# Attention of the first 512 tokens in chunks of 64 tokens, with its state kept on TensorE

## The chip, the cores and the metric

The kernel runs on one core of one Trainium2 chip. The metric is the device time of one execution in microseconds, taken as the median of several runs. The kernel before takes 574.92 us (three runs, 574.86 to 575.62).

## The reference

A linear attention with a decay per head (2 batch entries, 8 heads, 768 tokens, head size 64) gives 1536 rows of 512 features. Two wide layers follow (512 to 2048 to 512), the first with an ELU, the second with a rational function of the hidden value.

```python
for b in range(nb):                      # blocks of 64 tokens
    intra = einsum('bhic,bhjc->bhij', qb, kb) * Dmask      # lam**(i-j) for i >= j, else 0
    intra = einsum('bhij,bhjd->bhid', intra, vb)
    inter = einsum('bhid,bhde->bhie', qb * lam_pow, kv_state)
    out[:, :, sl] = intra + inter
    kv_state = lam_block * kv_state + einsum('bhsd,bhse->bhde', kb * rev_pow, vb)
x = out.transpose(0, 2, 1, 3).reshape(B * S, H * D)
x = elu(x @ w_in) @ w_out
h = x @ w2_in;  P = a0 + a1 h + a2 h^2 + a3 h^3;  Q = 1 + |b0||h| + |b1| h^2
y = (P / (Q + 1e-6)) @ w2_out
```

## The kernel before

The 1536 tokens are three tiles of T = 512. For each layer and tile, 16 slices f of 128 hidden features are computed: `mlp_h` (line 441) makes the hidden slice `h` with 12 products of 512 columns, `mlp_y` (line 523) adds it to the four output sums `y` with 12 more. Each operand is split into a high and a low part, and the three products high·high, high·low and low·high are summed, so `x` exists as `xhi` and `xlo`, and a weight as `w[:, 0]` and `w[:, 1]`. The split is a copy on ScalarE (line 57) and a subtraction on VectorE (line 58).

Attention is done twice over. For tiles 1 and 2 it runs inside the first layer: at chosen slices f (`visits`) `sm_products` does one chunk of 64 tokens between two groups of MLP products, with 64x64 operands in the tile names `aa`. For tile 0 it runs ahead of everything, in eight groups (c, g): c is one of four chunks of 128 tokens, g one of two groups of four heads. Per group TensorE makes the scores (`att_s`, line 209), and in `att_av` the products with the values (line 241), with the state (line 247) and the new state (line 254). GpSimd scales keys and queries (`att_kq`, lines 214 and 220), VectorE multiplies the scores by the decay mask (line 226), adds to the state (line 284) and makes `xlo` (line 277); ScalarE writes `xhi` (lines 263 and 269) and fades the state (line 266). `att_hand` (line 293) moves the state to the other half of the partitions for the later chunks.

Everything up to the third tile is written inside `manual_schedule`, so each engine runs its instructions in the order of the code. Loads are issued on SyncE (SP) in code order: the 16 pieces of queries, keys and values (line 192, 256 KB each) with the raw weight halves (line 114) between them. The raw weights are 64-bit floats, which VectorE narrows in three steps (lines 78, 81, 84); then they are split (lines 127 and 128). `idle` issues products of zeros on TensorE.

At the turn from tile 0 to tile 1, ScalarE stands in this order: the last chunk's output (line 390), the fade of the next chunk's keys (line 371, in `sm_decay_k`), a weight split (line 127), and the four splits of the new `x` (line 57), which the first `mlp_h` of tile 1 needs.

Of the kernel before, what the change touches and what calls it, by code (L numbers as in the profile page):

```python
# [29 lines left out]
def fused_kernel(ctx, tc, lam, qkv, w1, w2, ab, out):  # L30
# [132 lines left out]
    def make_w2(f, i):  # L163
# [5 lines left out]
        else:  # L169
# [5 lines left out]
    group = {}  # L175

    VIEWS = ("p (a x i) -> p a x i", "p (a x e) -> p a x e",
             "p (h a i) -> p h a i", "p (x a i) -> p x a i")

    def att_tile(c, g, j):  # L180

        b = group.setdefault((c, g), {})
        if j not in b:
            if j == 0:
                b["all"] = slot(2 + len(group) - 1, [P, 4, DM], F32, f"att{c}_{g}")
            b[j] = b["all"][:, j].rearrange(
                VIEWS[j], **({"h": 2, "a": 2} if j == 2 else {"a": 2, "x": 2}))
        return b[j]

    def att_load(c, g, parts=(0, 1)):  # L190
        for j in parts:
            nc.sync.dma_start(out=att_tile(c, g, j).rearrange("p a x i -> p (a x i)"),  # L192
                              in_=qkv[c, g, j])

    def psum_tiles(psum, name):
        return [pool.tile([P, T], F32, tag=tag, name=f"pa{h2}_{name}")
                .rearrange("p (a i) -> p a i", a=4) for h2, (pool, tag) in enumerate(psum)]

    def att_psum(c, g, psum):
        group[c, g]["ps"] = psum_tiles(psum, f"{c}_{g}")  # L200

    def att_s(c, g, psum):
        if "ps" not in group[c, g]:
            att_psum(c, g, psum)
        qk, ps = group[c, g][0], group[c, g]["ps"]
        for a in range(2):
            for h2 in range(2):
                r = slice(h2 * D, (h2 + 1) * D)
                nc.tensor.matmul(ps[h2][:, a], lhsT=qk[r, a, 1], rhs=qk[r, a, 0],  # L209
                                 start=True, stop=True)  # L210

    def att_kq(c, g):
        qk, kv, kq = group[c, g][0], att_tile(c, g, 1), att_tile(c, g, 3)
        nc.gpsimd.tensor_tensor(
            out=kq[:, 0].rearrange("p a (h d) -> p a h d", h=2),
            in0=kv[:, :, 0].rearrange("p a (h d) -> p a h d", h=2),
            in1=dmask[:, 4 * g:4 * g + 4, C - 1:C].rearrange("p (a h) i -> p a h i", h=2)
            .to_broadcast([P, 2, 2, D]), op=ALU.mult)
        if c:
            nc.gpsimd.tensor_tensor(out=kq[:, 1], in0=qk[:, :, 0], in1=qpow[:, 2 * g:2 * g + 2],  # L220
                                    op=ALU.mult)

    def att_mask(c, g):
        s, ps = att_tile(c, g, 2), group[c, g]["ps"]
        for h2 in range(2):
            nc.vector.tensor_tensor(
                out=s[:, h2], in0=ps[h2][:, 0:2],
                in1=dmask[:, 4 * g:4 * g + 4, 0:C].rearrange("p (a h) i -> p h a i", h=2)[:, h2],
                op=ALU.mult)

    def att_av(c, g):
        b = group[c, g]
        kv, s, kq, ps = b[1], b[2], b[3], b["ps"]
        first, last = c == 0, c == NC - 1
        pu = ps[1][:, 2].rearrange("p (a e) -> p a e", a=2)


        for a in range(2):
            for h2 in range(2):
                r = slice(h2 * D, (h2 + 1) * D)  # L240
                nc.tensor.matmul(ps[0][r, 2 + a], lhsT=kv[:, a, 1, r], rhs=s[:, h2, a],  # L241
                                 start=a == 0, stop=first, skip_group_check=True)
        if not first:
            for a in range(2):
                for h2 in range(2):
                    r = slice(h2 * D, (h2 + 1) * D)
                    nc.tensor.matmul(ps[0][r, 2 + a], lhsT=state[:, 2 * g + a, h2],  # L247
                                     rhs=kq[:, 1, a], start=False, stop=True,
                                     skip_group_check=True)
        for a in range(2):  # L250
            for h2 in range(2):
                r = slice(h2 * D, (h2 + 1) * D)
                ro = slice((1 - h2) * D, (2 - h2) * D) if last else r
                nc.tensor.matmul(pu[ro, a], lhsT=kq[:, 0, a, r], rhs=kv[:, a, 1, r],  # L254
                                 start=a == 0 or not last, stop=not last, skip_group_check=True)
        js = slice(c * C, (c + 1) * C)

        if c == 0:
            x_tiles(0, 0, g)
        hi, lo = xg[0, 0, g]  # L260
        gs_ = slice(2 * g, 2 * g + 2)
        if last:
            nc.scalar.activation(out=hi[:, :, js], in_=ps[0][:, 2:4], func=AF.Copy)
        if not first:
            for a in range(2):
                nc.scalar.activation(out=state[:, 2 * g + a], in_=state[:, 2 * g + a],
                                     func=AF.Copy, scale=qpow[:, 2 * g + a, C - 1:C])
        if not last:
            nc.scalar.activation(out=hi[:, :, js], in_=ps[0][:, 2:4], func=AF.Copy)
        if first:  # L270
            for h2 in range(2):
                r = slice(h2 * D, (h2 + 1) * D)
                nc.scalar.activation(out=state[r, gs_, h2, :], in_=pu[r], func=AF.Copy)

    def att_low(c, g):
        js, ps, (hi, lo) = slice(c * C, (c + 1) * C), group[c, g]["ps"], xg[0, 0, g]
        nc.vector.tensor_tensor(out=lo[:, :, js], in0=ps[0][:, 2:4],
                                in1=hi[:, :, js].bitcast(F32), op=ALU.subtract)

    def att_add(c, g):  # L280
        pu = group[c, g]["ps"][1][:, 2].rearrange("p (a e) -> p a e", a=2)
        for h2 in range(2):
            r = slice(h2 * D, (h2 + 1) * D)
            nc.vector.tensor_tensor(out=state[r, 2 * g:2 * g + 2, h2, :], in0=pu[r],
                                    in1=state[r, 2 * g:2 * g + 2, h2, :], op=ALU.add)

    def att_hand(c, g):

        pu = group[c, g]["ps"][1][:, 2].rearrange("p (a e) -> p a e", a=2)
        for a in range(2):  # L290
            for h2 in range(2):
                ro = slice((1 - h2) * D, (2 - h2) * D)
                nc.tensor.matmul(pu[ro, a], lhsT=ident, rhs=state[:, 2 * g + a, h2],  # L293
                                 start=False, stop=True, skip_group_check=True)
        nc.scalar.activation(out=state[:, 2 * g:2 * g + 2, 0], in_=pu, func=AF.Copy)

# [5 lines left out]

    def sm_load_qk(k):

        c, row = k // 2, 4 * P  # L310
        qk = qq.tile([P, NP, 2, C], F32, tag="qk", name=f"qk{c}")
        src = qkv[c, 0, 0]
        for rho, r in enumerate(ROWS):
            nc.sync.dma_start(
                out=qk[r].rearrange("p (g a) x i -> p g (a x i)", a=2),
                in_=bass.AP(src.tensor, src.offset + (1 - rho) * D * row,
                            [[row, D], [2 * P * row, NP // 2], [1, row]]))
# [14 lines left out]

    def sm_products(n, d):
# [40 lines left out]
    def sm_decay_q(n):  # L374
        q = chunk[n]["q"]
        if n % KB:
            nc.gpsimd.tensor_tensor(out=q, in0=q, in1=qpow[:, :, 0:CS], op=ALU.mult)

    def sm_mask(n):
        b = chunk[n]  # L380
        b["s"] = s = ap_.tile([P, NP, CS], F32, tag="s", name=f"s{n}")
        nc.vector.tensor_tensor(out=s, in0=aa_tiles[0][:, 0], in1=mask64[:, :, 0:CS], op=ALU.mult)
# [29 lines left out]
    def x_tiles(layer, t, g):  # L412
        key = f"{layer}_{t}_{g}"
        pool = xp if layer == 0 or t % 2 else xq
        xg[layer, t, g] = [pool.tile([P, 2, T], F32R, tag=f"x{w}{g}", name=f"x{w}{key}")
# [4 lines left out]
    def x_split(layer, t, m):  # L420
        with tc.high_priority(HP):
            if m % 2 == 0:
                x_tiles(layer, t, m // 2)
# [467 lines left out]
```

## Time and profile before

| | us |
|---|---|
| median of three runs | 574.92 |
| the profiled execution, its own time | 575.37 |
| its span, first to last instruction | 573.6 |
| start of the first MLP product (line 441) | 23.21 |
| TensorE busy in the span | 566.7 |

The span is read in two parts. Up to 23.21 us the core works on the attention of tile 0; behind that TensorE runs MLP products without a gap worth naming until near the end. The granted TensorE clock reads 1.00 over the whole span. A time on the page is of one instruction's whole length, and products overlap, so the distance from one start to the next tells the rate and not the length. A product in full fp32 is two instructions on TensorE in the trace, so 16 steps are 8 products of the code.

### The profile page before, as it was taken

The numbers are of one execution on the slowest core, as the hardware profiler recorded it, in microseconds if no ns is written. First come the engines' busy times: TensorE is split into PE (matmuls) and PEld (weight loads), VectorE is DVE, ScalarE is ACT, GpSimd is POOL, SyncE is SP. The second block draws the span as 40 slices with busy tenths as digits, with TensorE's granted clock in tenths as the row PEclk, the third lists the DMA queues.
The fourth block names the chain that finished last, engine by engine and source line by source line (L and its number), as shares of the span: only waits on it lengthen the run. The fifth ranks groups of instructions, "written<-read, shape, count | busy, mean of one in ns | idle before, by whom it ended". The sixth has DMA issues, their size and how long they took to land.

```text
span 573.6 us, 9267 instructions
## 1 busy us (share of the span) xinstructions
PE 566.7 (99%) x3554; PEld 465.8 (81%) x3554; DVE 467.6 (82%) x730; ACT 356.7 (62%) x682; POOL 27.5 (5%) x51
## 2 busy tenths in 40 slices
PE   7999999999999999999999999999999999999997
PEld 6878888878888888888888888888888888888885
DVE  6999999965586626877979999888898888898882
ACT  2565645865454445556568977667886676776672
POOL 6300000100010000000000000000000000000000
PEclk9999999999999999999999999999999999999999
DMA  8877687365778603544533400000300000200001
GB/s 296 274 237 260 209 251 221 83 164 161 221 216 244 185 11 125 183 142 156 175 99 103 162 22 2 0 1 1 129 18 2 0 1 0 75 0 2 0 1 74
DMA packets 41215, 64.58 MB, mean 113 GB/s; under 512 B 20178, under 2 KB 20178, under 8 KB 41170
## 3 DMA queue, kind: packets, MB, share of 16 engines
q1 hardware_dynamic: 41170, 63.98, 35.5%
q8 instruction: 28, 0.46, 0.3%
q14 instruction: 17, 0.14, 0.1%
HBM read 53.48 MB, written 10.49 MB: 112 GB/s over the span
## 4 chain that ended last, share of the span: by engine, by line
PE 97%; DMA 1%; SPq 1%; issue 0%; ACT 0%
PE h L441 46%; PE y L523 43%; PE y L432 3%; PE aa L346 1%; DMA att<-qkv_in 1%; PE aa L357 1%; SPq L192 1%; PE pa L241 1%; PE pa L247 1%; PE pa L209 0%; PE aa L362 0%; PE aa L351 0%; PE pa L254 0%; PE pa L293 0%; ACT o L493 0%
## 5 line engine op out<-in xcount | busy, mean ns | idle before, releaser
L441 PE MATMUL h<-xhi,w 128*128 128x512 f32 x768 | 205.7, 390 | 0.1
L523 PE MATMUL y<-ghi,w 128*128 128x512 f32 x712 | 191.8, 392 | 0.0
L441 PEld LDWEIGHTS h<-xhi,w 128*128 128x128 f32 x768 | 143.9, 188 | 31.2 <-ACT xhi L57 1.3
L523 PEld LDWEIGHTS y<-ghi,w 128*128 128x128 f32 x712 | 132.3, 188 | 27.8
L441 PE MATMUL h<-xlo,w 128*128 128x512 f32 x384 | 102.7, 389 | 0.0
L523 PE MATMUL y<-glo,w 128*128 128x512 f32 x356 | 95.3, 389 | 0.0
L441 PEld LDWEIGHTS h<-xlo,w 128*128 128x128 f32 x384 | 72.1, 188 | 15.2 <-DVE xlo L58 0.2
L523 PEld LDWEIGHTS y<-glo,w 128*128 128x128 f32 x356 | 66.8, 188 | 14.2
L467 ACT ACTIVATE a<-h,babs 128x512 f32<-128x512 f32 x48 | 33.0, 688 | 63.9 <-PE h L441 63.7
L454 ACT ACTIVATE a<-h 128x512 f32<-128x512 f32 x48 | 28.2, 589 | 48.3 <-PE h L441 48.2
L471 DVE SCALAR_TENSOR_TENSOR b<-b,babs,a 128x512 f32<-128x512 f32 x48 | 36.0, 750 | 21.2 <-ACT b L468 21.1
L456 DVE SCALAR_TENSOR_TENSOR b<-a,h 128x512 f32<-128x512 f32 x48 | 32.7, 681 | 17.1 <-ACT a L455 14.1
L458 ACT ACTIVATE ghi<-b 128x512 fp32r<-128x512 f32 x48 | 30.0, 626 | 19.0 <-DVE b L456 19.0
L459 DVE TENSOR_TENSOR glo<-b,ghi 128x512 fp32r<-128x512 f32 x48 | 33.9, 708 | 7.0 <-ACT ghi L458 5.5
L469 ACT ACTIVATE p<-h,cab 128x512 f32<-128x512 f32 x48 | 37.6, 784 | 0.0
L473 ACT ACTIVATE a<-b,one 128x512 f32<-128x512 f32 x48 | 34.9, 728 | 3.2 <-DVE b L471 2.7
L475 DVE SCALAR_TENSOR_TENSOR p<-p,cab,h 128x512 f32<-128x512 f32 x48 | 35.8, 746 | 1.2
L479 DVE SCALAR_TENSOR_TENSOR b<-b,one,a 128x512 f32<-128x512 f32 x48 | 35.8, 746 | 0.1
L481 DVE SCALAR_TENSOR_TENSOR p<-p,cab,a 128x512 f32<-128x512 f32 x48 | 35.8, 746 | 0.0
L58 DVE TENSOR_TENSOR glo<-p,ghi 128x512 fp32r<-128x512 f32 x48 | 33.0, 687 | 3.1 <-PE y L432 1.5
L474 DVE TENSOR_TENSOR p<-p,h 128x512 f32<-128x512 f32 x48 | 32.7, 681 | 2.9 <-ACT p L469 2.9
L483 DVE SCALAR_TENSOR_TENSOR p<-b,p 128x512 f32<-128x512 f32 x48 | 33.1, 690 | 1.2
(87 smaller groups left out, 612.4 us busy)
## 6 DMA issues: line engine op xcount, KB each, us to landing
raw<-w_in SPq DMA_DIRECT2D x64, 512.0 KB, 4.3
att<-qkv_in SPq DMA_DIRECT2D x16, 256.0 KB, 5.8
qk<-qkv_in SPq DMA_DIRECT2D x16, 256.0 KB, 4.1
kv<-qkv_in SPq DMA_DIRECT2D x64, 64.0 KB, 3.9
w2d<-wbuf SPq DMA_DIRECT2D x16, 256.0 KB, 4.4
wbuf<-w2d SPq DMA_DIRECT2D x16, 256.0 KB, 2.7
x2d<-o SPq DMA_DIRECT2D x12, 256.0 KB, 2.2
x2r<-x2d SPq DMA_DIRECT2D x12, 256.0 KB, 3.1
```

The source lines that it names most:

```text
L58: lo_eng.tensor_tensor(out=lo, in0=src, in1=hi.bitcast(F32), op=ALU.subtract)
L441: nc.tensor.matmul(h, lhsT=w[:, a, 0, k * P:(k + 1) * P], rhs=xs[layer, t, k][b], start=i == k == 0, stop=i == 2 and k == NP - 1)
L459: lambda: nc.vector.tensor_tensor(out=glo, in0=b, in1=ghi.bitcast(F32), op=ALU.subtract)]
L467: nc.scalar.activation(out=a, in_=h, func=AF.Abs, scale=babs[:, 0:1])
L469: nc.scalar.activation(out=p, in_=h, func=AF.Identity, scale=cab[:, 3:4], bias=cab[:, 2:3])
L471: nc.vector.scalar_tensor_tensor(out=b, in0=b, scalar=babs[:, 1:2], in1=a, op0=ALU.mult, op1=ALU.add)
L473: nc.scalar.activation(out=a, in_=b, func=AF.Ln, bias=one[:, 0:1])
L475: nc.vector.scalar_tensor_tensor(out=p, in0=p, scalar=cab[:, 1:2], in1=h, op0=ALU.add, op1=ALU.mult)
L479: nc.vector.scalar_tensor_tensor(out=b, in0=b, scalar=one[:, 0:1], in1=a, op0=ALU.add, op1=ALU.mult)
L481: nc.vector.scalar_tensor_tensor(out=p, in0=p, scalar=cab[:, 0:1], in1=a, op0=ALU.add, op1=ALU.mult)
L483: nc.vector.scalar_tensor_tensor(out=p, in0=b, scalar=2.0, in1=p, op0=ALU.subtract, op1=ALU.mult, reverse0=True)
L523: nc.tensor.matmul(ys[layer, t][m], lhsT=w[:, a, 1, m * P:(m + 1) * P], rhs=g[b], start=f == i == 0, stop=False)
```

## The change

The attention of tile 0 works in chunks of 64 tokens. One piece holds two chunks b = 0, 1 of all eight heads; its keys and values stand in opposite halves of the partitions. All products have 64x64 operands. The state is carried in PSUM: `att_kv` makes the new part, `att_fade` adds the old state times a diagonal `fade`, and ScalarE copies the sum out (`att_state`) for the next chunk. `att_inter` multiplies the state by the faded queries. Where products of different row halves write into one bank, `fence` makes the next product wait for a tiny ScalarE instruction (`mark`), which waits for the last product.

The loads come as eight pieces of 512 KB: queries and keys of c = 0, a raw weight half, the values of c = 0 and 1, and so on; the queries of c = 2 and 3 are last. The `x` tiles become one tile for all four feature groups. For the very first hidden slice the order of the parts is high·high, low·high, high·low. The tables of powers are made on GpSimd (`make_qpow` twice), so the two products of line 339 and `pick` go. `att_hand` goes: the last `att_fade` does its work. At the turn to tile 1 the fade of the keys is issued behind the splits of `x`.

```diff
-            for r in ROWS:
-                nc.tensor.matmul(aa_tiles[1][r, 1], lhsT=pick[r], rhs=mask64[r, :, 1:CS + 1],
-                                 start=True, stop=True, skip_group_check=True)
-            nc.scalar.activation(out=qpow[:, :, 0:CS], in_=aa_tiles[1][:, 1], func=AF.Copy)
...
+    def mark():
+        i = nc.scalar.activation(out=marks[0:1, 0:1], in_=one[0:1], func=AF.Copy)
+        order(i, pe["last"])
+        return i
+    def fence(i):
+        pe["after"] = i
...
+    def att_kd(c):
+        t = att[c]
+        for g in range(2):
+            gm = slice(2 * g, 2 * g + 2)
+            nc.gpsimd.tensor_tensor(
+                out=t["kd"][:, gm].rearrange("p m (h d) -> p m h d", h=2),
+                in0=t["kv"][:, gm, 0].rearrange("p m (h d) -> p m h d", h=2),
+                in1=dmask[:, 4 * g:4 * g + 4, CS - 1:CS].rearrange("p (m h) i -> p m h i", h=2)
+                .to_broadcast([P, 2, 2, D]), op=ALU.mult)
+    def att_qd(c, b, eng):
+        t, j = att[c], slice(b * CS, (b + 1) * CS)
+        eng.tensor_tensor(out=t["qd"][:, :, j], in0=t["qk"][:, :, 0, j], in1=qnat, op=ALU.mult)
+    def att_av(c, bs=(0, 1)):
+        t = att[c]
+        for m in range(NP):
+            for h2, e in enumerate(ROWS):
+                for b in bs:
+                    att_mm(t["px"][b][e, m], lhsT=t["kv"][ROWS[1 - b], m, 1, e],
+                           rhs=t["s"][ROWS[1 - b], h2, m], start=False, stop=c > 0 or b == 0)
+    def att_kv(c):
+        t = att[c]
+        for m in range(NP):
+            for h2, e in enumerate(ROWS):
+                for b in (1, 0):
+                    o = ROWS[1 - h2] if (c, b) == (NC - 1, 1) else e
+                    att_mm(t["pu"][b][o, m], lhsT=t["kd"][ROWS[1 - b], m, e],
+                           rhs=t["kv"][ROWS[1 - b], m, 1, e], start=m == 0, stop=c == b == 0)
+    def att_inter(c, b):
+        t, p = att[c], plane(2 * c + b)
+        for m in range(NP):
+            for r in ROWS:
+                att_mm(t["px"][b][r, m], lhsT=p[r, m], rhs=t["qd"][r, m, b * CS:(b + 1) * CS],
+                       start=False, stop=not c)
+    def att_fade(c, b):
+        t, p = att[c], plane(2 * c + b)
+        for m in range(NP):
+            for i, r in enumerate(ROWS):
+                att_mm(t["pu"][b][ROWS[1 - i] if (c, b) == (NC - 1, 1) else r, m],
+                       lhsT=fade[r, m], rhs=p[r, m], start=False, stop=True)
+    def att_state(c, b):
+        return nc.scalar.activation(out=plane(2 * c + b + 1), in_=att[c]["pu"][b], func=AF.Copy)
...
+            att_kd(0); att_qd(0, 1, G); att_av(0); att_hi(0, 0); att_low(0, 0)
+            idle(2); att_kv(0); idle(1); att_state(0, 0)
...
+            att_inter(0, 1); att_fade(0, 1); att_state(0, 1); att_hi(0, 1)
...
+            att_s(1, ms); att_mask(1, 0); att_mask(1, 1); att_low(0, 1)
+            att_qd(1, 0, G); att_qd(1, 1, V); att_kv(1)
+            fence(mark())
+            att_fade(1, 0); att_inter(1, 0); att_state(1, 0); att_kd(2)
+            att_fade(1, 1); att_inter(1, 1); f = att_state(1, 1)
+            att_av(1, (0,)); fence(f); att_av(1, (1,)); att_hi(1, 0); att_hi(1, 1)
...
+            att_kv(2); fence(mark()); att_fade(2, 0); att_state(2, 0)
+            att_kv(3); att_fade(2, 1); att_state(2, 1)
+            att_qd(2, 0, G); att_qd(2, 1, V); att_s(2, ms[:2])
+            att_inter(2, 0); att_inter(2, 1); att_s(2, ms[2:])
+            att_mask(2, 0); att_mask(2, 1); att_fade(3, 0); att_state(3, 0)
...
+            att_s(3, ms); att_mask(3, 0); att_mask(3, 1); att_av(2); att_hi(2, 0); att_hi(2, 1)
...
+            att_inter(3, 0); att_inter(3, 1); fence(mark())
+            att_av(3); att_hi(3, 0); att_hi(3, 1); att_low(3, 0); att_low(3, 1)
...
                     for m in range(NP):
                         x_split(0, t, m)
+                    for n in due:
+                        sm_decay_k(n)
...
                     for n in due:
-                        sm_decay_k(n)
+                        if f < NF - 1:
+                            sm_decay_k(n)
```

(Several calls stand on one line here.) The next two excerpts are of TensorE, in the middle of the attention of tile 0; names that begin with `pa` or `ps` are sums in PSUM, `att` are tiles in SBUF. First before, from the products of the group (2, 0) on:

```order
L241 MATMUL pa_2_0_305<-att_0_178 64x128 x4
L247 MATMUL pa_2_0_305<-att_0_178,state 64x128 x4
L254 MATMUL pa_2_0_306<-att_0_178 64x64 x4
L209 MATMUL pa_3_1_392<-att_1_188 128x128
L209 MATMUL pa_3_1_393<-att_1_188 128x128
L209 MATMUL pa_3_1_392<-att_1_188 128x128
L209 MATMUL pa_3_1_393<-att_1_188 128x128
L241 MATMUL pa_2_1_333<-att_1_180 64x128 x4
```

Now the change, behind `att_kv(1)`: fade and inter of chunk (1, 0), the same of (1, 1), and the two halves of `att_av(1)`.

```order
L213 MATMUL ps_2_323<-att_0_138,att_2_142 64x64 x8
L213 MATMUL ps_2_323<-att_1_140,att_0_138 64x64 x8
L213 MATMUL ps_3_324<-att_1_140,att_2_142 64x64 x8
L213 MATMUL ps_3_324<-att_1_140 64x64 x8
L213 MATMUL ps_2_323<-att_1_140,att_1_139 64x64 x8
L213 MATMUL ps_3_324<-att_1_140,att_1_139 64x64 x8
```

Groups of four products with 128 columns, whose state is added elsewhere, become groups of eight products with 64 columns; the second row's sum stands in the bank of the first, and the third row reads the state that comes out of it.

ScalarE at the turn from tile 0 to tile 1, before:

```order
L390 ACTIVATE xr_764<-aa_614 128x4x64
L371 ACTIVATE kv_1445<-kv_1445,dmask 128x64 x4
L127 ACTIVATE w_15_235<-wbuf 128x512
L57 ACTIVATE xhi_1_0_1568<-xr_764 128x512 x2
L57 ACTIVATE xhi_1_1_1574<-xr_764 128x512 x2
L458 ACTIVATE ghi_0_15_1475<-b_0_15_1478 128x512
```

And now (`xr` is the attention's output, `kv` the loaded keys and values):

```order
L400 ACTIVATE xr_920<-aa_773 128x4x64
L127 ACTIVATE w_15_229<-wbuf 128x512
L57 ACTIVATE xhi_1_1720<-xr_920 128x512 x4
L381 ACTIVATE kv_1601<-kv_1601,mask_164 128x64 x4
L467 ACTIVATE ghi_0_15_1631<-b_0_15_1634 128x512
```

The four fades of the keys, which wait for a load, have moved from ahead of the splits to behind them.

## Rows read from the trace of the kernel before

**Rows 1.** The page: busy time by engine, and the chain by line.

```profile
PE 566.7 (99%) x3554; PEld 465.8 (81%) x3554; DVE 467.6 (82%) x730; ACT 356.7 (62%) x682; POOL 27.5 (5%) x51
PE h L441 46%; PE y L523 43%; PE y L432 3%; PE aa L346 1%; DMA att<-qkv_in 1%; PE aa L357 1%; SPq L192 1%; PE pa L241 1%; PE pa L247 1%; PE pa L209 0%; PE aa L362 0%; PE aa L351 0%; PE pa L254 0%; PE pa L293 0%; ACT o L493 0%
```

**Rows 2.** The chain in order of time (start, length, what) to 39 us.

```profile
28.95 0.38 PE pa L293 x8
...
32.27 2.72 PE y L523 x12
34.99 2.89 PE h L441 x12
...
38.47 0.46 PE aa L346 x16
```

**Rows 3.** Timeline of TensorE (start, length, operation, shapes, count, idle before).

```profile
4.76 2.08 PE L209 MATMUL pa<-att 64*128 64x128 f32 x16
...
8.18 0.72 PE L209 MATMUL pa<-att 64*128 64x128 f32 x8
...
22.54 0.27 PE L247 MATMUL pa<-att,state 128*64 128x128 f32 x1
...
23.21 1.20 PE L441 MATMUL h<-xhi,w 128*128 128x512 f32 x4
```

**Rows 4.** Timeline of GpSimd, the scaled keys and queries.

```profile
7.61 0.62 POOL L214 TENSOR_TENSOR att<-att,dmask 128x256 f32<-128x256 f32 x1 [0.19 <-DMA att<-qkv_in]
9.56 0.62 POOL L214 TENSOR_TENSOR att<-att,dmask 128x256 f32<-128x256 f32 x1 [1.33 <-DMA att<-qkv_in]
...
15.00 0.61 POOL L214 TENSOR_TENSOR att<-att,dmask 128x256 f32<-128x256 f32 x1
15.58 0.72 POOL L220 TENSOR_TENSOR att<-att,qpow 128x256 f32<-128x256 f32 x1
```

**Rows 5.** Timeline of ScalarE at the end of the attention of tile 0.

```profile
21.55 0.38 ACT L263 ACTIVATE xhi<-pa 128x256 fp32r<-128x256 f32 x1 [0.72 <-PE pa L247]
21.83 0.69 ACT L266 ACTIVATE state<-state,qpow 128x128 f32<-128x128 f32 x2
22.85 0.39 ACT L263 ACTIVATE xhi<-pa 128x256 fp32r<-128x256 f32 x1 [0.34 <-PE pa L247]
...
25.15 0.19 ACT L693 ACTIVATE babs<-cab 128x2 f32<-128x2 f32 x1
```

**Rows 6.** Timeline of TensorE around the visits at 38 and 114 us.

```profile
37.82 0.65 PE L339 MATMUL aa<-dmask,tabs 64*64 64x256 f32 x4
38.30 0.63 PE L346 MATMUL aa<-qk 64*64 64x64 f32 x16
...
113.59 0.27 PE L346 MATMUL aa<-qk 64*64 64x64 f32 x2
...
114.53 0.23 PE L362 MATMUL aa<-qk,state 64*64 64x64 f32 x2
```

**Rows 7.** The chain in order of time at the turn to tile 1.

```profile
120.42 0.34 PE h L441
...
121.83 4.20 PE h L441 x17
```

**Rows 8.** Timelines of ScalarE and, last row, VectorE at the turn to tile 1.

```profile
115.78 0.37 ACT L390 ACTIVATE xr<-aa 128x256 f32<-128x256 f32 x1
118.11 1.07 ACT L371 ACTIVATE kv<-kv,dmask 128x64 f32<-128x64 f32 x4 [1.96 <-DMA kv<-qkv_in]
...
119.60 2.18 ACT L57 ACTIVATE xhi<-xr 128x512 fp32r<-128x512 f32 x4
...
120.25 2.50 DVE L58 TENSOR_TENSOR xlo<-xr,xhi 128x512 fp32r<-128x512 f32 x4 [3.38 <-ACT xhi L57]
```

**Rows 9.** Windows: busy by engine (TensorE, loads, VectorE, ScalarE, GpSimd), granted clock, DMA.

```profile
4.00:8.00 4.00, 4.00 (x36) 3.41 (x35) 3.74 (x11) 0.12 (x1) 3.28 (x9) 1.00 0.93 286
8.00:12.00 4.00, 2.25 (x34) 1.80 (x32) 2.88 (x7) 1.51 (x6) 2.67 (x5) 1.00 1.04 401
```

More of the change, by code (lines that the diff above doesn't have):

```diff
@@ L190, in att_load @@
[L190 to L295, printed above, removed]
     CS = D
@@ L331, in sm_load_kv, with att_mm, order @@
                     [[row, CS], [P, 4], [1, D]]))
+    att = []
+    pe = {"last": None, "after": None}
+    def att_mm(out, **kw):
+        i = nc.tensor.matmul(out, skip_group_check=True, **kw)
+        if pe["after"] is not None:
+            order(i, pe["after"])
+        pe.update(last=i, after=None)
+    def order(i, j):
+        tc.add_manual_dep(i.ins, j.ins.name,
+                          mybir.DependencyInfo(mybir.DependencyClass.Sync, mybir.DependencyReason.DATA),
+                          reason="row tiles of one bank")
@@ new lines, in att_psum, with att_s @@
+    def att_psum(c):
+        pools = (((ph, "h"), (ph, "h"), (pa, "pa0"), (pa, "pa1")), ((py, "y"),) * 4)[c % 2]
+        ps = [pool.tile([P, T], F32, tag=tag, name=f"ps{c}_{i}")
+              .rearrange("p (x m i) -> p x m i", x=2, m=NP) for i, (pool, tag) in enumerate(pools)]
+        x = 2 if c else 0
+        att[c].update(ps=[ps[i][:, 0] for i in range(2)], pu=[ps[2 + i][:, 0] for i in range(2)],
+                      px=[ps[i + x][:, 1] for i in range(2)])
+    def att_s(c, ms):
+        t = att[c]
+        for m in ms:
+            for b in range(2):
+                for h2, r in enumerate(ROWS):
+                    att_mm(t["ps"][h2][ROWS[1 - b], m], lhsT=t["qk"][r, m, 1, (1 - b) * CS:(2 - b) * CS],
+                           rhs=t["qk"][r, m, 0, b * CS:(b + 1) * CS], start=True, stop=True)
@@ L555, in fused_kernel @@
+        dmask = att[3]["spare"].rearrange("p (h i) -> p h i", h=H)
+        fade = att[2]["spare"].rearrange("p (x m i) -> p x m i", x=2, m=NP)[:, 0]
+        qnat = att[2]["spare"].rearrange("p (x m i) -> p x m i", x=2, m=NP)[:, 1]
+        ident = ap_.tile([P, NP, CS], F32, tag="s", name="ident")[:, 0]
         for last in (D - 1, P - 1):
-            nc.gpsimd.affine_select(out=pick, in_=pick, pattern=[[0, D]], base=-last,
+            nc.gpsimd.affine_select(out=diag, in_=diag, pattern=[[1, CS]], base=-last,
@@ L625, in run, with idle @@
                         ops.pop(0)()
-            att_psum(*atts[0], pp[0])
-            idle(3, group[atts[0]]["ps"])
-            pl = group[atts[0]]["ps"][0][:, 3, 0:H]
-            nc.tensor.matmul(pl, lhsT=zero[0:1, P:2 * P], rhs=lam1, start=True, stop=True)
+            x_tiles(0, 0)
+            att_psum(0)
+            spare = py.tile([P, T], F32, tag="y", name="spare")
+            def idle(n, out=spare):
+                for _ in range(n):
+                    nc.tensor.matmul(out[:, 0:P], lhsT=zero[:, 0:P], rhs=zero[:, 0:P],
+                                     start=True, stop=True, skip_group_check=True)
@@ L631, in fused_kernel @@
+            idle(3)
+            pl = spare[:, P:P + H]
+            nc.tensor.matmul(pl, lhsT=zero[0:1, P:2 * P], rhs=lam1, start=True, stop=True,
+                             skip_group_check=True)
             nc.vector.tensor_copy(out=lamb, in_=pl)
[L632 removed]
+            idle(3)
             for h in range(H):
                 make_decay(h)
[L635 to L640 removed]
@@ L675, in fused_kernel @@
-            s_part(7)
-            masks(7)
-            av(5)
-            add(5)
-            low(5)
-            av(6)
-            low(6)
-            run(c1, 1)
-            av(7)
-            low(7)
-            run(c1, 2)
-            att_hand(*atts[6])
+            V, G, ms = nc.vector, nc.gpsimd, range(NP)
+            att_s(0, ms)
+            att_mask(0, 0)
+            att_mask(0, 1)
+            idle(5)
+            run(c0, 3)
+            att_kd(0)
+            att_qd(0, 1, G)
+            att_av(0)
@@ new lines, in fused_kernel @@
+            att_hi(0, 0)
+            att_low(0, 0)
+            idle(2)
+            att_kv(0)
+            idle(1)
+            att_state(0, 0)
+            run(c0, 1)
+            att_kd(1)
+            att_inter(0, 1)
+            att_fade(0, 1)
+            att_state(0, 1)
+            att_hi(0, 1)
+            run(c0, 1)
+            att_psum(1)
+            att_s(1, ms)
+            att_mask(1, 0)
+            att_mask(1, 1)
+            att_low(0, 1)
+            att_qd(1, 0, G)
+            att_qd(1, 1, V)
@@ new lines, in fused_kernel @@
+            att_kv(1)
+            fence(mark())
+            att_fade(1, 0)
+            att_inter(1, 0)
+            att_state(1, 0)
+            att_kd(2)
+            att_fade(1, 1)
+            att_inter(1, 1)
+            f = att_state(1, 1)
+            att_av(1, (0,))
+            fence(f)
+            att_av(1, (1,))
+            att_hi(1, 0)
+            att_hi(1, 1)
+            run(c1, 3)
+            att_low(1, 0)
+            att_low(1, 1)
+            att_kd(3)
+            att_psum(2)
@@ new lines, in fused_kernel @@
+            att_kv(2)
+            fence(mark())
+            att_fade(2, 0)
+            att_state(2, 0)
+            att_psum(3)
+            att_kv(3)
+            att_fade(2, 1)
+            att_state(2, 1)
+            att_qd(2, 0, G)
+            att_qd(2, 1, V)
+            att_s(2, ms[:2])
+            att_inter(2, 0)
+            att_inter(2, 1)
+            att_s(2, ms[2:])
+            att_mask(2, 0)
+            att_mask(2, 1)
+            att_fade(3, 0)
+            att_state(3, 0)
@@ new lines, in fused_kernel @@
+            run(c1, 1)
+            att_qd(3, 0, G)
+            att_qd(3, 1, V)
+            att_s(3, ms)
+            att_mask(3, 0)
+            att_mask(3, 1)
+            att_av(2)
+            att_hi(2, 0)
+            att_hi(2, 1)
+            run(c1, 1)
+            att_low(2, 0)
+            att_low(2, 1)
+            att_inter(3, 0)
+            att_inter(3, 1)
+            fence(mark())
+            att_av(3)
+            att_hi(3, 0)
+            att_hi(3, 1)
+            att_low(3, 0)
```

198 lines of the change are left out of this document (92 added, 106 removed).

## The prediction

> **What bounds the kernel now.** I read the page first: TensorE is busy for 566.7 of 573.6 us, and the chain that ended last is nearly all MLP products [rows 1]. So only two things can move the end: when the first MLP product starts, and holes in the row of products behind it. Next I read the chain in order of time. The first MLP product starts at 23.21 [rows 3], and behind it the chain is products on TensorE alone, the hand's and the visits' among them [rows 2]. Then the timelines of that first stage engine by engine: TensorE [rows 3], GpSimd [rows 4] and ScalarE [rows 5]. The reader is to see that GpSimd waits there for pieces of the load, and that TensorE, at the stage's end, waits on turns through ScalarE. Then the visits [rows 6] and the turn to tile 1 [rows 7, 8]. There ScalarE stands 1.96 us before the faded keys, waiting for their load, while the splits of `x` stand behind them. Last the granted clock by window [rows 9].
>
> **The scale.** The profiled execution took 575.37, 1.77 over its span and 0.45 over the median of 574.92. I sum on 575.37 and take 0.45 off. This kernel's measurement can't tell a difference below 0.2% (1.15 us) from none.
>
> **Part 1: the attention of tile 0.** It is now one long queue on TensorE, and I work out its end S, which is the start of the first MLP product, against 23.21.
>
> *When it can start.* Scores of c = 0 need only the first load. The first link that holds up the queue is `att_kv(0)`, which needs the faded keys. Before, GpSimd waits for the fourth 256 KB piece of the load until 7.61 and for the seventh until 9.56 [rows 4]: 0.65 us a piece. Now the values of c = 0 come behind the queries (two pieces' bytes) and a raw half (two more), so they are complete with the sixth piece's bytes: 9.56 - 0.65 = 8.9. A raw half has longer lines, and if lines and not bytes set the pace, it counts as one piece: 8.3. The keys' fade is two GpSimd instructions of 128x256: 0.58 from one start to the next and 0.62 for the last [rows 4], with 0.05 to hand it on: 1.25. The queue starts at 10.15 by bytes and at 9.55 by lines.
>
> *The products.* A visit's 16 steps of 64x64, eight products in fp32 on two quarters of the array, take 0.46 [rows 2]. A visit of 64 steps, which uses all four quarters, starts its first two at 113.59 and its last two at 114.53 [rows 6]: 0.94 for 62, so 0.48 for 32 steps, 16 products. A group thus costs 0.47, whether it is eight products on two quarters or 16 on four. Behind the start I count 24 such groups ahead of the first MLP product: one `att_kv` for c = 0 to 3 (4), `att_inter` of seven chunks (7), `att_fade` of six (6), `att_s` of c = 1 to 3 (3), `att_av` of c = 1 in two halves and of c = 2 and 3 (4). 24 x 0.47 = 11.3.
>
> *The turns.* Where TensorE needs what ScalarE makes of the last product, it stands. From the start of a last product to ScalarE is 22.54 to 22.85 [rows 3, 5]: 0.27 length and 0.04 hand-over; I take 0.16 for the shorter 64-column product. A copy of 128x256 from PSUM takes 0.38, with 0.28 to the next start [rows 5]; 0.05 back to TensorE. A state turn is then 0.16 + 0.04 + 0.38 + 0.05 = 0.63. A mark is a tiny instruction, as the 0.19 of 128x2 [rows 5]: 0.16 + 0.04 + 0.19 + 0.05 = 0.44. By the order of the code these lie on the path: the states of (0, 0) and (1, 0), bare, 1.26; the first and the last mark 0.88; the middle mark with the copies of `xhi` that stand ahead of it on ScalarE 0.55; the fence on the state of (1, 1), half covered by a half `att_av`, 0.25; the state of (2, 0) behind `att_kv(3)` and the masks of c = 3 behind VectorE's other work, 0.1 each; and the last pair of `xhi` copies, which the first MLP product waits for, 0.16 + 0.04 + 0.28 + 0.38 + 0.05 = 0.91. Sum 4.05. The other turns lie under products of another chunk. If all but the last pair and two state turns were hidden, it would be 2.2.
>
> S = 10.15 + 11.3 + 4.05 = 25.5 by bytes, 24.9 by lines; I take the middle, 25.2. The bounds: 9.55 + 11.3 + 2.2 = 23.1 (by lines, turns hidden), and 26.4 (by bytes, with GpSimd's fade a quarter slower, +0.3, and as much, +0.6, on the 2.5 of ScalarE's work in the turns, as both go on beside VectorE's narrowing). The queries of c = 2 and 3, though loaded last, come before 19 by the same pace; they are not needed until some 18 to 20. So part 1 costs +2.0, bounds -0.1 and +3.2.
>
> At the marks a rule speaks against the change. Rows 6 show no wait for ScalarE within a visit, so on rows alone a mark could cost nothing where its product has drained. The Trainium skill ("TensorEngine Tiling (Array Packing)", Restrictions and Gotchas) says that row tiles can't use one PSUM bank at the same time and that the program has to keep them apart. By it the three marks are needed and cost up to 3 x 0.44 = 1.3; without it S could be 1.3 lower, which lies inside the bounds above.
>
> **Part 2: what is saved later.** The products of line 339 stand on TensorE's path at 37.82, and the visit starts at 38.30 [rows 6]: -0.48. The tables that replace them are made on GpSimd behind the attention, needed at the first visit some 13 us later; GpSimd is busy 27.5 us of the span [rows 1], which hides them (bare, ten instructions of at most 0.62 [rows 4] would be 6.2). The second slice's third group of products took 2.89 for 2.72 [rows 2], a wait for a weight: with a later start of the products, VectorE's narrowing is ahead of them, -0.17. The hand's eight steps of 0.38 [rows 2] become a fade of 16 steps: +0.09.
>
> At the turn to tile 1 the chain shows 20 products from 120.42 to 126.03 (three alone, then 17) [rows 7]: 5.61, where 20 at 2.72 / 12 take 4.53 [rows 2]: a hole of 1.08. ScalarE's splits there start at 119.60, behind the keys' fade that waited for its load until 118.11 [rows 8]. With the fade behind them they follow the output of 115.78 and one weight split, two microseconds earlier; TensorE needs them at 120.42, so the hole goes: -1.08. Next late is the gelu's copy behind the fade; with four fades of 1.07 in all it is ready within the slice's 5.4 us, so I cost the new place at 0 (if the load came 2 us later still, up to +0.5).
>
> Larger loads move the same bytes and one order of parts in the first slice takes no product away: 0, within -0.2 and +0.3.
>
> **Sum.** +2.0 - 0.48 - 0.17 + 0.09 - 1.08 = +0.36: 575.7 on the profiled scale, 575.3 by the median.
>
> **The rivals.**
>
> *B, the turns hide, faster.* If TensorE finds other products in nearly every turn, S is near its lower bound, say 23.4, and the sum +0.2 - 1.64 = -1.44: 573.5. For it: the 11.3 of products has independent groups, and before, the chain is mostly load and TensorE. Against it: the state goes from chunk to chunk eight times in series, each through ScalarE.
>
> *C, doubled products, slower.* Before, 16 steps of 64x128 at 4.76 take 2.08, and at 8.18 eight take 0.72 [rows 3], 0.21 against 0.11 a pair of starts, although the granted clock of both windows reads 1.00, the level of 2.4 GHz [rows 9]. If the early rate lasts until about 13 because the new first stage waits more than it works, the four groups `att_inter`, `att_fade`, `att_s` and `att_kv` there take 0.94 for 0.47: +1.9, 577.2. It decides if products started after 9 still take the doubled time. Against it: at 8.18 the rate had already changed, in a window in which TensorE was busy for only 2.25 of 4 us [rows 3, 9]. The Trainium skill ("TensorE: Matmul & The Clock Gate", Part 1) says that the clock starts at half and that work releases it, and idling takes it back; the row of the granted clock does not show a half level here, so the rule has only the doubled steps for it.
>
> *D, the move at the turn does nothing*, because the splits now wait for the weight split and VectorE's narrowing ahead of it: the hole stays, +1.08, 576.4. Against it: VectorE sat idle for 3.38 before its part of the splits, waiting for ScalarE [rows 8], so its narrowing was done.
>
> **Chances.** Forecast 0.48. B 0.25, from the lower bound of the turns. C 0.13. D 0.05. The upper end of part 1 (S above 25.9) 0.09, which is slower too. So faster 0.25, same 0.48, slower 0.27. The range runs from 573.4, B's time with a little more, to 577.1, just short of C; the forecast's own is 574.4 to 576.1.
>
> **What would show it.** The first product of an MLP slice at 25.2 (B: 23.4; C: 27). GpSimd's first fade of keys at 8.3 to 8.9. Gaps of TensorE of about 0.4 ahead of the products behind the three marks, and of 0.6 behind the copies of the states of (0, 0) and (1, 0). Groups of 64x64 at 0.47 from 10 us on (C: 0.94 until 13). No product ahead of the first visit's scores. Slice 0 of tile 1 with 12 products in 2.72, and its splits before 119. I am wrong if the first MLP product comes before 24 or after 26.5, or if a new hole opens behind it.

## The result and the profile after

The kernel got slower, clear of noise. The prediction of 575.3 us, with a range from 573.4 to 577.1, missed it.

| | before | after |
|---|---|---|
| median of four runs, us | 575.04 | 583.50 |
| ratio of after to before, 95% interval | | 1.0133 (1.0113 to 1.0153) |
| span of the profiled execution, us | 573.6 | 581.6 |
| start of the first MLP product, us | 23.21 | 32.06 |
| from there to the first product of tile 1, us | 97.06 | 96.70 |
| the 24 products of the first two slices of tile 1, us | 6.51 | 5.99 |
| from there to the end, us | 443.19 | 443.19 |

The last four rows add up to the end of the last product, some 3.6 us ahead of the span's end in both. Behind the first MLP product the change gains 0.36 and 0.52, where 0.56 and 1.08 were forecast. Ahead of it the change loses 8.85, where +2.0 was forecast. So nearly all that went wrong happened in the first 32 us.

The chain in order of time tells where. These are pieces of it in the changed kernel (start, length, what; "issue" is time in which the engine waited for nothing that the profile shows):

```profile
10.59 0.02 issue
...
10.67 0.39 ACT att L331
11.07 0.14 issue
11.20 2.05 PE ps L213 x91
13.25 1.55 issue
14.80 0.23 PE ps L213
15.03 0.02 issue
15.05 0.21 ACT marks L226
15.26 0.04 issue
15.30 1.89 PE ps L213 x32
...
17.71 2.12 PE ps L213 x44
...
21.01 0.08 issue
21.09 0.28 PE ps L213
...
22.93 2.08 PE ps L213 x72
25.02 2.33 issue
27.35 2.58 PE ps L213 x110
...
30.71 0.10 issue
30.81 0.52 PE ps L213 x15
31.33 0.02 issue
31.35 0.67 ACT xhi L339 x2
32.02 0.04 issue
32.06 0.97 PE h L450 x3
```

The reader is to see two long pieces with no releaser, 1.55 and 2.33, and two short ones that end at 21.09 and 30.81, all inside rows of products. The ones that end at 14.80 and 21.09 stand just ahead of the product that a mark waits for, so this view alone does not tell whether they belong to the marks; the run pad below does. The turns are a little longer than forecast: the state turn takes 0.61 from the end of its last product at 10.59 to 11.20, where the forecast 0.63 counts 0.16 of that product too and so leaves 0.47, and the first mark takes 0.50 from 14.80 to 15.30 (0.44 was forecast).

What the four places have in common appears when the span is cut there and TensorE's instructions are counted (windows of the changed kernel: stretch, length, then busy time and instructions of TensorE's products, of its weight loads, of VectorE, ScalarE and GpSimd, granted clock, DMA share, GB/s):

```profile
0.00:14.79 14.79, 11.67 (x221) 10.26 (x222) 8.64 (x25) 3.23 (x6) 10.37 (x27) 1.00 0.84 318
14.79:21.09 6.29, 5.36 (x128) 4.69 (x127) 1.76 (x4) 1.74 (x5) 4.31 (x11) 0.73 1.04 399
21.09:27.34 6.25, 3.50 (x127) 3.08 (x127) 1.19 (x3) 0.97 (x3) 1.34 (x4) 1.00 0.82 155
27.34:30.81 3.47, 3.01 (x127) 2.73 (x128) 2.78 (x7) 1.76 (x5) 0.00 (x0) 1.00 0.02 5
```

Products and loads of the last three stretches are 255, 254 and 255; with the few waits for semaphores that the trace lists among them, each comes to 256, and the first stretch to 449. TensorE stands each time that 256 instructions are through, at the counts 449, 705, 961 and 1217. A product in full fp32 is two weight loads and two products here, four instructions, so the chunks need 1244 products and loads ahead of the first MLP product. Before, it is 524:

```profile
0.00:23.20 23.20, 19.98 (x262) 17.61 (x262) 17.90 (x49) 8.72 (x25) 14.77 (x36) 1.00 0.93 326
```

Instructions are data too, and come by DMA. This is the table of queues of the changed kernel's whole execution (packets, MB, share):

```profile
q1 hardware_dynamic: 41042, 63.98, 34.9%
q8 instruction: 30, 0.49, 0.4%
q14 instruction: 16, 0.13, 0.1%
```

TensorE's 7886 traced instructions over the 30 packets of q8 are 263 a packet, and a packet is 16 KB, so q8 is taken to be TensorE's queue. In the trace such a packet starts at 12.46, 18.53, 24.23 and 28.54, always behind the passing of one of the counts (193 at 9.87, then 14.80, 21.09, 27.34), and TensorE goes on some 1.2 to 1.6 us after the packet's end. So it looks as if a block is asked for when the block two before it is used up; it is there 4.9, 6.3, 6.25 and 3.5 us later. The last of them, without other loads, is the short one. The Trainium skill ("Runtime: NRT & Kernel Launch", Instruction fetch mechanics) states blocks of 256 instructions, fetched over a queue while the one before runs; the counts agree. It gives TensorE room for 2048 instructions and calls the cost of a block's end mostly hidden; here TensorE stood at its instruction 449, and the measurement decides.

The clock is a second effect of the same stalls. The first stage of the changed kernel by windows, same columns:

```profile
12.00:14.00 2.00, 1.25 (x75) 1.15 (x72) 2.00 (x5) 0.66 (x2) 1.93 (x3) 1.00 1.03 377
16.00:18.00 2.00, 1.46 (x29) 1.28 (x28) 0.08 (x1) 0.38 (x1) 1.83 (x3) 0.50 1.05 410
18.00:20.00 2.00, 1.98 (x52) 1.84 (x51) 0.00 (x0) 0.51 (x2) 1.35 (x5) 0.78 1.04 391
```

After the stall of 1.55 the granted clock falls from 1.00 to 0.50, the level of 1.2 GHz. The 32 steps from 15.30 take 1.89; the same 32 take 1.15 in the run hold_pad below, at the full clock. It cost little here, since the next block came only at 21.09. (A window shows the clock only where the trace has a record of it. The records begin at 8.63 here and at 7.29 before; a window without a record reads 1.00.)

### The profile page after: what moved, and what is told of

Read it like the earlier page. It is cut to its first block, busy times and chain, and to the rows that moved or that the text cites. A ratio compares the mean times of both kernels' runs of the same rounds, so it can differ in the third digit from the quotient of the medians.

```text
span 581.6 us, 9939 instructions
## 1 busy us (share of the span) xinstructions
PE 570.0 (98%) x3918; PEld 469.4 (81%) x3918; DVE 463.4 (80%) x717; ACT 354.6 (61%) x674; POOL 31.3 (5%) x56
## 4 chain that ended last, share of the span: by engine, by line
PE 98%; issue 1%; ACT 1%; DVE 0%; ACTq 0%
PE h L450 45%; PE y L532 42%; PE y L441 3%; PE ps L213 3%; PE aa L356 1%; PE spare L626 1%; PE aa L367 1%; PE aa L372 0%; PE aa L361 0%; ACT att L331 0%; ACT xhi L339 0%; ACT marks L226 0%; ACT o L502 0%; PE spare L631 0%; DVE lamb L633 0%
```

## Experiments

The ratios are to the runs of before on the same chip, with their 95% interval; pad, hold and hold_pad have two runs each.

| run | time, us | ratio to before | first MLP product, us |
|---|---|---|---|
| turn_only | 573.89 | 0.9976 (0.9966 to 0.9985) | 22.71 |
| better | 573.63 | 0.9969 (0.9958 to 0.9980) | 22.80 |
| attention_only | 585.48 | 1.0181 (1.0164 to 1.0198) | 32.62 |
| half | 576.50 | 1.0018 (1.0008 to 1.0028) | 25.27 |
| pad | 585.70 | 1.0171 (1.0123 to 1.0219) | 35.63 |
| hold | 584.52 | 1.0151 (1.0108 to 1.0194) | 30.65 |
| hold_pad | 581.87 | 1.0113 (1.0079 to 1.0147) | 28.83 |

**The move at the turn alone (turn_only).**

```diff
 # before.py
+                    for n in due:          # behind the x_split calls of tile 1
+                        sm_decay_k(n)
...
                     for n in due:
-                        sm_decay_k(n)
+                        if f < NF - 1:
+                            sm_decay_k(n)
```

> The attention of before, with only the move at the turn to tile 1: the keys' fade behind the splits of x. Theory (by the prediction's step): the hole at the first slice of tile 1 goes whole, -1.08, so 573.9. Rival (by what the profile after shows at its turn, where the weight split still stands ahead of the splits of x and starts at 127.03 behind VectorE's narrowing): about half of the hole stays, -0.5, so 574.5.

Measured: 573.89, the theory's 573.9. To the last digit this is luck: before on the same chip took 575.31, 1.42 more, and in the profile the first MLP product came 0.50 earlier than before (22.71), which the edit does not touch. The turn itself shows what the edit did. ScalarE and TensorE there, from two timelines of this run:

```profile
115.29 0.37 ACT L390 ACTIVATE xr<-aa 128x256 f32<-128x256 f32 x1
116.42 0.63 ACT L127 ACTIVATE w<-wbuf 128x512 fp32r<-128x512 f32 x1 [0.76 <-DVE wbuf L84]
116.95 2.18 ACT L57 ACTIVATE xhi<-xr 128x512 fp32r<-128x512 f32 x4
119.03 1.05 ACT L371 ACTIVATE kv<-kv,dmask 128x64 f32<-128x64 f32 x4
```

```profile
119.77 1.07 PE L441 MATMUL h<-xhi,w 128*128 128x512 f32 x4
120.68 1.07 PE L441 MATMUL h<-xlo,w 128*128 128x512 f32 x4
```

The splits start at 116.95 and not at 119.60 [rows 8], and four products take 0.91 from start to start, where [rows 7] show 1.41 for three, from 120.42 to 121.83. The 24 products take 5.44 instead of 6.51: 1.07 gained, where the step said 1.08.

**The same, with the weight split behind the splits too, and the table of line 339 on GpSimd (better).**

```diff
 # before.py, with the edit of turn_only
                     for m in range(NP):
                         x_split(0, t, m)
+                    run(lows, 1)
...
-                    run(w, len(w) - 1)
+                    run(w, len(w) - 1 - (t == 0 and f == NF - 1))
...
-            for r in ROWS:
-                nc.tensor.matmul(aa_tiles[1][r, 1], lhsT=pick[r], ...)
...
+            make_qpow(CS, True)            # GpSimd, behind the attention
```

> The attention of before; at the turn to tile 1 the splits of x stand ahead of both the weight split and the keys' fade, and the table of line 339 is made on GpSimd instead of by products on TensorE. Theory: the hole at the turn goes (-0.9) and the 0.48 of line 339 too: 573.6. Rival: the weight split, now late, or the new table on GpSimd opens a hole of its own behind, and the time stays at 574.5 to 575.

Measured: 573.63. It beats both kernels, but not turn_only beyond the noise. The products of line 339 are gone: from the first MLP product to tile 1 it takes 96.84 instead of 97.06, so 0.22 of the 0.48. The rest went to other places of that stretch, which was not followed further. The turn is 5.44 as with turn_only, so the weight split ahead of the splits cost nothing there.

**The attention alone (attention_only).** The reverse edit, on the changed kernel.

```diff
 # after.py
-                    for n in due:          # behind the x_split calls of tile 1
-                        sm_decay_k(n)
...
                     for n in due:
-                        if f < NF - 1:
-                            sm_decay_k(n)
+                        sm_decay_k(n)
```

> The changed kernel with the keys' fade at the turn back in its old place. Theory (the loss is all in the attention of tile 0, and the move at the turn is worth about half of its hole): 584.0, the first MLP product at 32 as in the profile after. Rival (the move is worth its whole 1.08): 584.6. If the loss came from the turn, this would be near 576.

Measured: 585.48, more than either expectation, with the first MLP product at 32.62. The loss is the attention's, as the theory says; the move was mis-sized by it. The turn takes 6.52, as before, and the stretch from the first MLP product to tile 1 is 0.73 longer than in the profile after, so the move is worth 0.53 + 0.73 = 1.26 in this kernel; another 0.56 is the later first MLP product. TensorE stands at the same counts, but the stalls are 1.82, 1.32, 1.46 and 0.65 long, and the clock falls at another place:

```profile
18.00:20.00 2.00, 1.55 (x58) 1.27 (x54) 0.86 (x3) 1.13 (x3) 1.57 (x6) 1.00 1.04 388
20.00:22.00 2.00, 0.76 (x11) 0.62 (x12) 0.37 (x1) 0.20 (x1) 1.71 (x6) 0.79 1.04 364
22.00:24.00 2.00, 2.00 (x62) 2.00 (x64) 0.00 (x0) 0.38 (x1) 0.10 (x1) 0.50 1.10 179
```

Here the clock is 1.00 where the changed kernel had 0.50 (16 to 18), and 0.50 where that had 1.00, and yet the blocks come at 14.59, 20.89, 27.35 and 31.37, as there within some 0.2, but for the last, which is 0.56 later. The chain of blocks sets the length, not the clock.

**Half as many products (half).**

```diff
 # after.py, in att_av, att_kv, att_inter, att_fade (att_s: ms[::2]); sums and moving operands take m:m + 2
-        for m in range(NP):
+        for m in range(0, NP, 2):
...
-                att_mm(t["px"][b][r, m], lhsT=p[r, m], rhs=t["qd"][r, m, b * CS:(b + 1) * CS],
+                att_mm(t["px"][b][r, m:m + 2], lhsT=p[r, m], rhs=t["qd"][r, m:m + 2, b * CS:(b + 1) * CS],
```

> The changed kernel with half as many products in the attention of tile 0: each makes 64x128 instead of 64x64, using the weights of every other feature group for two, so the attention's values are others; columns, copies, marks and waits stay. Theory (TensorE's instructions come too late: in the profile after it stands at its instructions 449, 705, 961 and 1217, which are 256 apart): with some 640 instead of 1250 instructions ahead of the first MLP product, no idle time without a releaser over 0.5 us is left, the clock doesn't fall, and the first MLP product starts at 22.5 to 25.5 instead of 32.06. Rival (the fences, marks and turns through ScalarE make the length): all of these stay, at most half of the 11.3 us of products goes, and the first MLP product starts at 26.5 or later, with the two stalls of 1.55 and 2.33 still at the first mark and ahead of the fade of chunk (3, 0).

Measured: 576.50, the first MLP product at 25.27. Its windows up to there, and its first MLP products:

```profile
0.00:25.26 25.26, 20.96 (x326) 17.32 (x326) 14.68 (x38) 8.40 (x22) 16.32 (x41) 1.00 0.93 322
```

```profile
25.27 2.11 PE L450 MATMUL h<-xhi,w 128*128 128x512 f32 x8 [0.76 <-ACT xhi L339]
```

The same columns, copies, marks and waits, with 652 products and loads instead of 1244, end 6.8 us sooner: no stall without a releaser is left, and the clock stays 1.00. So the marks and turns, which are all still there, are not what made the 6.9 by which the forecast missed. It also shows that even in this shape, with instructions in time, the chunks of 64 gain nothing: 1.0018 of before.

**More instructions ahead (pad).**

```diff
 # after.py
-            idle(5)
+            for i in range(32):
+                nc.tensor.matmul(spare[ROWS[i % 2], 0:16], lhsT=zero[ROWS[0], 0:CS], rhs=zero[ROWS[0], 0:16],
+                                 start=True, stop=True, skip_group_check=True)
```

> The changed kernel with 32 small products of zeros (64x64 on 16 columns) in the place of the five idle products behind the first scores: 108 more instructions on TensorE ahead of the rest. Theory (TensorE stands at its instructions 449, 705, 961 and 1217, whatever these are): the stalls come at the same four counts, which now lie 108 instructions earlier in the program (among the scores of c = 1, the values' products of c = 1, the first scores of c = 2, the end of the values' products of c = 2), and no longer at the first mark and ahead of the fade of chunk (3, 0). Each lasts until 5 to 6.5 us after the count 256 lower was passed, the last one 3.5 to 4; the first MLP product starts at 31 to 33.5, as the chain of these is as long. Rival (the stalls belong to the marks and the sums that share a bank): they stay at the same products as in the profile after.

Measured: 585.70. TensorE stands at the counts, not at the places of the program. Of the four stalls that were expected two came, at 705 and 961; at 449 and 1217 the block was in time. The two stalls and the windows up to them:

```profile
20.16 1.18 PE L213 MATMUL ps<-att,att 64*64 64x64 f32 x55 [1.45 <-issue]
27.64 0.49 PE L213 MATMUL ps<-att 64*64 64x64 f32 x8 [3.90 <-issue]
```

```profile
0.00:20.15 20.15, 16.27 (x349) 14.74 (x350) 11.29 (x26) 4.20 (x9) 13.66 (x34) 1.00 0.93 339
20.15:27.63 7.48, 3.12 (x127) 2.71 (x127) 1.19 (x3) 1.63 (x5) 2.35 (x8) 0.89 0.86 181
```

699 products and loads and a few waits stand ahead of the first, 254 and two waits between the two. The stall at the first mark is gone, because the block for 449 had been asked for sooner (193 was passed at 8.46). The size was missed: the first MLP product comes at 35.63 and not by 33.5. The block behind 20.16 took 7.5 us, and during the 3.90 without instructions the clock fell to 0.50, for the windows from 26 to 32. Behind 27.64 no block was late, so there the half clock did lengthen the stage.

**Loads behind the attention's held back (hold).**

```diff
 # after.py
-            load_pair(0)                   # and cab, load_pair(1), the first loads of tile 1
...
             att_state(3, 0)
+            hold.append(pe["last"])        # the next load waits for this product
+            load_pair(0)                   # and the others
```

> The changed kernel with the loads behind the attention's (the first two pairs of raw weights, 3 KB of coefficients, the first loads for the chunks of tile 1) held back until the last product of the fade of chunk (3, 0). Theory (the instructions of TensorE come by DMA and queue with these loads, so what is held back makes them come sooner): the first two stalls stay as in the profile after (until 14.8 and 21), the third block comes 3.5 to 4.5 us after 21 instead of 6.25, so the stall of 2.33 at count 961 falls under 0.7, and the first MLP product starts at 29 to 30.5 instead of 32.06 (the MLP behind it may then wait for its weights). Rival (a block takes its 6.3 us whatever else is loaded): 32.

Measured: 584.52, the first MLP product at 30.65. The two blocks whose fetch met little or no other load, by windows that are cut where a block begins:

```profile
15.25:22.37 7.12, 6.28 (x127) 5.88 (x128) 1.46 (x4) 1.74 (x5) 5.71 (x14) 0.53 0.16 55
22.37:26.08 3.71, 3.24 (x135) 2.95 (x130) 0.70 (x2) 0.97 (x3) 0.00 (x0) 0.98 0.02 4
```

Past the first stall (1.82, with all loads running) no block is late any more: the one at 961 is there by 26.08, 3.71 after 705 was passed, where the changed kernel took 6.25. The packets start at 16.45 and 22.82, 1.2 and 0.5 behind the counts, where the changed kernel's started 3.7 and 3.1 behind them. So the loads do hold up the instructions. The expectation was missed by 0.15 in the first product's start, since now the clock counts: it is 0.50 from 16 to 22, and 256 instructions take 7.12 without a stall. The MLP behind waits 2.5 for its weights, so the total hardly moves.

**Both (hold_pad).** The edits of pad and hold in one kernel.

> The changed kernel with both the 32 small products of zeros ahead (so that the first block of instructions is asked for sooner) and the loads behind the attention's held back (so that the later blocks come sooner). Theory (the time lost ahead of the MLP is stalls for instructions, and the fall of the clock that follows a stall): the stall at count 449 is gone as with the zeros alone, the later blocks come within 4 us, so no stall without a releaser over 0.7 us is left, the granted clock stays 1.00 in every window from 8 us on, and the first MLP product starts at 26.5 to 28, which is the 25.27 of the kernel with half the products plus the 1.7 by which the zeros delay the first keys' product. Rival (the clock falls because TensorE waits at marks and state turns, whatever its instructions do): the clock falls again and the product starts at 30 or later.

Measured: 581.87, the first MLP product at 28.83, 0.8 later than expected. The three blocks behind 449:

```profile
14.92:19.09 4.17, 3.29 (x138) 3.02 (x133) 3.47 (x7) 1.25 (x4) 2.69 (x4) 1.00 0.34 125
19.09:22.91 3.82, 3.33 (x133) 2.92 (x132) 1.99 (x4) 1.74 (x5) 3.23 (x11) 1.00 0.02 4
22.91:25.71 2.80, 2.80 (x141) 2.80 (x136) 1.18 (x4) 1.11 (x3) 0.35 (x1) 1.00 0.02 6
```

No stall over 0.1 without a releaser is left, and the clock does not fall, with the same marks and state turns on the path. So the marks and turns alone do not drop the clock; in these runs it fell only with a stall for instructions. Of the 1352 products and loads here none is late, and the stage is 3.2 us shorter than in the changed kernel although it has 108 more of them. The time gains only 1.6, because behind it the MLP waits for its weights: from the first MLP product to tile 1 it takes 98.60.

The 0.8 by which it is late has a likely source at the start. The clock's records begin here only at 14.55 us, and ahead of that the products run at half pace. The same 16 steps, in the changed kernel and here:

```profile
11.20 0.68 PE L213 MATMUL ps<-att 64*64 64x64 f32 x16 [0.24 <-ACT att L331]
```

```profile
13.35 1.12 PE L217 MATMUL ps<-att 64*64 64x64 f32 x16
```

Pairs of steps are 0.107 apart up to 14.5 and 0.059 behind it, so the clock was most likely still at half, in windows that read 1.00. From the first product with the faded keys to the last row of products ahead of the first mark it takes 3.72 (11.56 to 15.28), where the changed kernel takes 2.75 (9.85 to 12.60): 0.97 lost. The products of zeros thus did more than shift the counts; in pad, too, the records begin only at 12.32.

## Why the prediction was wrong

- **The step that failed** is "A group thus costs 0.47", with "one long queue on TensorE": it priced columns and turns, and took the instructions for free. I read 0.47 off visits that stand alone between MLP slices, where 32 or 128 instructions come after a slice of 24 that lasts 2.72. The price itself holds where instructions are in time: in hold_pad the 32 steps of two groups, from 16.30, take 1.15, of which the last step's own length is 0.22, so 0.93 against 0.94. But with 24 such groups in a row, TensorE uses a block of 256 in about 3 us, and the next one is there only after 3.5 to 6.3. From the first product with the faded keys to the first MLP product the sum has 11.3 + 4.05 = 15.35; the changed kernel took 22.21 (9.85 to 32.06), and hold_pad, with no block late, 17.27 (11.56 to 28.83), of which 0.97 is the half pace at its start. So late blocks and the half clock behind them made some 5.9 of the 6.9 that were missed; of the last 0.9 a part is the longer turns, the rest stays open. The page of before showed the queue's row, and the trace its instruction packets; neither was read.
- **The rest of part 1 was near, in part by luck.** The products with the new state started at 9.85, between the 9.55 and 10.15 of the sum, but by two misses that cancel: the keys' fade began at 7.59, earlier than forecast, and took 1.1 an instruction and not 0.6. With half as many instructions the first MLP product came at 25.27, against 25.2; that kernel's first product with the faded keys started at 9.16, so its queue took 16.11 and not 15.35. The turns were 0.61 and 0.50, against 0.47 and 0.44 counted alike. The marks, against which a rule of tiling had been weighed, were neither free nor the problem.
- **Rival C** (doubled products) was weighed with a reading that is none: the records of the clock begin at 7.29 before, so the 1.00 of the window from 4 to 8, like the 1.00 over the whole span, is not a reading of the time ahead of that. The early doubled pace was most likely the half clock, as at the start of hold_pad. It did not last until 13: in the changed kernel the records begin at 8.63, at 1.00, and products from 9 us on ran at the full rate. The half clock came back only after a stall (pairs of steps 0.107 apart from 15.3 to 18.6), and in attention_only it came at another place without shortening or lengthening the stage much. So C named the right sign, but did not happen as written.
- **Part 2** was right in size for the move at the turn, alone: -1.07 against -1.08. In the changed kernel only 0.52 of it shows against before, and 1.26 against its own attention with the old order. There the splits began at 127.57, 1.19 ahead of TensorE, since the weight split ahead of them waited for VectorE until 127.03; turn_only had 2.8 to spare. That is rival D in part. It is not fixed by the change: in pad and hold_pad, with the same order, the 24 products took 5.44, the whole gain. The line 339 and the weight's wait gave back 0.36 of the 0.56 that was forecast: the fade behind the first slice added about 0.2 and not 0.09 (16 steps from 37.43 to 38.36, 0.93 from the last MLP product before to the next, where the hand had 0.70 from 28.56 to 29.26).
- The chance of 0.27 for slower held none of this: all rivals moved S by at most 2 us, because all of them kept TensorE fed with instructions.

## What to carry to other kernels

Count the instructions of a stage, not only its columns: where small products follow one another for more than 256 instructions, ask how soon the next block can be there, and read the rows of the instruction queue and the "issue" pieces of the chain. Four instructions for a 64x64 fp32 product that lasts 0.03 to 0.06 us are too many while bulk loads run; wider products of the same columns need half as many. And when two edits travel together, run each alone: here the small one gained 0.24% and the large one lost 1.8%.

## What the runs showed of the hardware

- In the changed kernel TensorE stood at its instructions 449, 705, 961 and 1217, 256 apart, and went on 1.2 to 1.6 us after a 16 KB packet of the instruction queue had ended. Counted from the passing of the count 256 lower, late blocks were there after 4.9 to 7.5 us with bulk loads running (after, attention_only, pad, hold), and after 3.5 and 4.0 with the DMA idle (after, attention_only). With the loads held back none was late in hold_pad, where TensorE used up its blocks in 2.8 to 4.2.
- The granted clock fell from 1.00 to 0.50 after or during a stall, and products went on at 0.50 for a while: from 15.5 to 18.9 after 1.55 (after), from 21.2 to 24.6 after 1.32 (attention_only), from 15.7 to 22.5 after 1.82 (hold), from 26.0 to 32.8 during 3.90 (pad). It did not fall after each stall: 2.33 in after, 1.82 in attention_only and 1.45 in pad left it at 1.00.
- The records of the clock began at 7.1 us in half, 8.6 in after, 12.3 in pad and 14.6 in hold_pad; products ahead of that ran at half pace, in windows that read 1.00.
- The same columns in products of 64x128 instead of twice as many of 64x64 made this stage 6.8 us shorter.
